# A MoBA attention and MoE MLP kernel: the written-out order of its operations, its buffer picks and its engine choices replaced

## The chip, the cores and the metric

The kernel runs on one core of one Trainium2 chip. The metric is the device time of one execution in microseconds (us). The kernel before was run three times: 254.47, 254.54 and 254.04 us, median 254.47. Its engines are TensorE (PE; its weight loads are listed apart as PEld), VectorE (DVE), ScalarE (ACT), GpSimd (POOL) and SyncE (SP), which here only issues DMAs. Each engine works through its own instruction queue in order; an instruction that waits holds up everything behind it on that engine.

## The reference

The inputs are q, k and v of shape 4 x 8 x 768 x 64 (batch, head, position, width) and the weights w_in (512 x 2048) and w_out (2048 x 512). Per batch and head there is an attention in which each position sees its own block of 64 keys and the blocks among its three best, by the product of its query with the mean of a block's keys:

```
k_rep = k.reshape(B, H, 12, 64, D).mean(axis=3)
gate  = where(causal by block, q . k_rep, -1e9)
mask  = (block in the best 3 of gate, or own block) and key <= query
attn  = softmax(where(mask, q . k / 8, -1e9))
x     = (attn @ v), heads side by side: 3072 x 512
h     = x @ w_in
g     = 0.5 h (1 + tanh(c (h + 0.044715 h^3)))
out   = g @ w_out
```

## The kernel before

The 32 heads are worked on as 16 pairs, p = 0 to 15; pair p belongs to batch b = p // 4. The kernel first describes its whole work as operations, each of which issues one or a few instructions on one engine, with the operations it depends on and the buffers it takes. They get numbers in the order in which they are described. Three written-out tables then say what becomes of them: ORDER is the sequence of the numbers in which the operations are issued, which is thus each engine's sequence too; BUFFER picks, for each buffer taken, one of the copies of its kind; ENGINE lists the operations that run on another engine than the first that they name. This is done at L215 to L225:

```python
engine = {n: e for e, ops in ENGINE.items() for n in ops}
picks = iter(BUFFER)
for n in ORDER:
    op = self.ops[n]
    for kind, key in op.takes:
        if key not in self.buf:
            self.buf[key] = self.kinds[kind][0][next(picks)]
    op.emit(engine.get(n, next(iter(op.engines))))
```

No planner runs when the kernel is built: the three tables are the schedule.

The work of a pair runs as follows.

- **Loads.** load (L371 to L398) brings keys, queries and values by SP, in two transfers for batch 0 and for all values (L387), in four of 32 columns each for the keys and queries of batches 1 to 3 (L393). Pair 0 has its own form, load_0 (L414 to L421): keys on SP's queue, queries on ScalarE's, each in two halves. The values are cast to 16 bit by GpSimd (cast_v, L358).
- **Weights.** load_w (L445 to L453) brings w_in and w_out in two halves each, issued by GpSimd. The first of these issues stands behind a small copy (L451) that needs pair 3's values to have landed. A small transfer on SP (hold, L1560) keeps the loads of batch 1 behind the landing of w_in.
- **Turning.** In batch 0, TensorE transposes keys (L538) and queries (L541) through PSUM, and copies and casts bring them back. In the other batches VectorE transposes 32 x 32 blocks (tr, L557) and a cast (q16 and kc, L356 on ScalarE, L360 on VectorE, L358 on GpSimd) makes them 16 bit.
- **Gate.** VectorE sums the keys of each block (ks, L614; the product ksb, L588 or L631, places them for two heads), TensorE multiplies them with the queries (gate, L680), and VectorE picks the best three (L696 to L717). The result is turned by TensorE or by a DMA (L749, L756) and copied (mc) into twelve extra rows below the queries (76 rows in all), with marker rows below the keys (fill, L513).
- **Scores.** TensorE makes the scores (L856 in batch 0, L1039 else), ScalarE their exponentials (L875, L1052), GpSimd clears what is not causal (L901, L1066), TensorE multiplies with the values and a column of ones (L924, L1078), VectorE divides (L942 and L943, L961 and L962). TensorE turns the result (ot, L981; a DMA at L986 for some) and a copy, otc, puts it into xT.

The work of a batch after its attention is the first product s1 with w_in (L1115, two matmuls to an operation), the gelu on ScalarE (L1127) and the second product with w_out. In batch 0 the second product is plain (s2_plain, L1315; stored at L1340). In batches 1 to 3 it has the form of Strassen with seven products of halves (L1365), whose sums VectorE makes (L1284 for the weights, L1302) and joins (L1414; stored at L1449 and L1458). Batch 3's first product also has this form for three of its column groups (prod, L1204): a product lies in a wide buffer of PSUM, of which there are two; keep (L356, L360) copies one half out of it, and plus (L1163) adds the other.

Around these, ORDER weaves one batch's products into the next batch's attention. Matmuls of zeros (warm, L1517) stand in front of the first work and at chosen places further on. ScalarE changes its table between exponential and gelu (L822).

Of the kernel before, what the change touches and what calls it, by code (L numbers as in the profile page):

```python
# [182 lines left out]
    "POOL": [  # L183
        337, 586, 587, 646, 647, 707, 708, 972, 973, 1035, 1036, 1097, 1159,
        1160, 1425, 1426, 1488, 1489, 1551, 1613]}


class Op:
# [1431 lines left out]
```

## Time and profile before

| | |
|---|---|
| runs | 254.47, 254.54, 254.04 us; median 254.47 |
| profiled execution | 253.93 us, of which span (first to last instruction) 252.2 us |
| granted TensorE clock | 1.000 |
| TensorE | 244.2 us, 97% of the span, 2484 instructions |
| VectorE | 188.8 us, 75%, 535 |
| ScalarE | 177.5 us, 70%, 226 |
| GpSimd | 84.0 us, 33%, 166 |
| DMA | 32.62 MB, 129 GB/s on average |

The profile is of one execution. A timeline row gives the start in us from the start of the span, the duration, engine, line, operation, what it writes and reads, the tile shape of a matmul, sizes and how many instructions the row groups; in brackets stands the idle time of the engine before it and what ended it. Rows of TensorE overlap, since its matmuls are pipelined: what one costs is read from the start of one to the start of the next. A row of the groups by line gives the busy time and the mean of one in ns, then the idle time before them and what ended it. A row of the windows gives the busy time in one stretch, engine by engine, with the instructions in brackets.

### The profile page before, as it was taken

What the parts mean: (1) busy time and instruction counts of PE and PEld (TensorE: products, weight loads), DVE (VectorE), ACT (ScalarE), POOL (GpSimd) and SP (SyncE); (2) the same over time, 40 slices, a digit from 0 to 9 for tenths busy, and PEclk for the clock granted to TensorE, in tenths of its full rate; (3) what the DMA queues carried; (4) which work ended last, traced back from release to release, by engine and by line L of the source; (5) the groups of instructions that cost most, each with busy time, mean ns of one, the idle gap of its engine ahead of it and who ended that gap; (6) DMA issues with size and microseconds to landing.
All of it is one profiled execution on the core that took longest, in us unless ns stands there. A gap on an engine that the chain in (4) does not pass through costs nothing.

```text
span 252.2 us, 6437 instructions
## 1 busy us (share of the span) xinstructions
PE 244.2 (97%) x2484; PEld 170.2 (67%) x2484; DVE 188.8 (75%) x535; ACT 177.5 (70%) x226; POOL 84.0 (33%) x166
## 2 busy tenths in 40 slices
PE   6899999999999999999999999999999999999993
PEld 4677776555555565565778887656777887666883
DVE  2679851034789999999997998999876585688954
ACT  2498978545899899867899795576999936656200
POOL 8657860011237657112147561210147500000000
PEclk9999999999999999999999999999999999999999
DMA  7998699999989987999899667184121330100023
GB/s 159 218 200 184 97 213 198 205 156 151 153 140 164 155 170 127 146 138 261 151 182 162 137 109 140 27 214 99 26 86 28 90 120 30 65 22 0 4 106 144
DMA packets 130927, 32.62 MB, mean 129 GB/s; under 512 B 124528, under 2 KB 126928, under 8 KB 130896
## 3 DMA queue, kind: packets, MB, share of 16 engines
q1 hardware_dynamic: 126160, 27.62, 62.8%
q0 software_dynamic: 3136, 4.19, 9.8%
q10 hardware_dynamic: 1600, 0.39, 0.8%
q8 instruction: 19, 0.31, 0.5%
q14 instruction: 12, 0.10, 0.1%
HBM read 27.26 MB, written 6.29 MB: 133 GB/s over the span
## 4 chain that ended last, share of the span: by engine, by line
PE 80%; SPq 8%; DMA 4%; DVE 3%; POOL 2%; issue 1%; DVEq 0%; POOLq 0%
PE wide L1115 27%; PE bank L1365 22%; PE wide L1039 9%; SPq L387 7%; PE bank L1315 6%; PE wide L1204 6%; PE bank L1078 5%; DMA vsd<-in_v_dram 2%; PE bank L680 2%; SPq L393 2%; DMA sd<-in_k_dram 1%; DMA G<-in_q_dram 1%; PE bank L924 1%; PE wide L856 1%; PE bank L981 1%
## 5 line engine op out<-in xcount | busy, mean ns | idle before, releaser
L1115 PE MATMUL wide<-xT,w_in 128*128 128x384 f16 x416 | 74.8, 326 | 0.0
L1052 ACT ACTIVATE ats<-wide 128x896 f16<-128x896 f32 x72 | 63.1, 915 | 5.8 <-PE wide L1039 3.8
L1127 ACT ACTIVATE G<-wide 128x768 f16<-128x768 f32 x52 | 42.0, 810 | 27.4 <-PE wide L1115 23.1
L1115 PEld LDWEIGHTS <-w_in 128*128 128x128 f16 x416 | 39.9, 98 | 26.9 <-issue 1.0
L1066 POOL TENSOR_SCALAR_AFFINE_SELECT ats<-ats 128x256 f16<-128x256 f16 x72 | 31.0, 443 | 51.1 <-ACT ats L1052 37.5
L1039 PE MATMUL wide<-qT,kT 76*128 76x512 f16 (+3 forms) x192 | 38.8, 305 | 0.0
L557 DVE STREAM_TRANSPOSE s<-sd 128x768 f32<-128x768 f32 x24 | 23.2, 971 | 14.2 <-DMA sd<-in_k_dram 12.9
L1365 PE MATMUL bank<-w_out,G 128*128 128x256 f16 x216 | 32.6, 272 | 0.0
L1365 PEld LDWEIGHTS <-G 128*128 128x128 f16 x288 | 26.9, 98 | 5.5
L1315 PE MATMUL bank<-w_out,G 128*128 128x512 f16 x96 | 28.8, 379 | 0.0
L358 POOL CAST kT<-s 64x768 f16<-64x768 f32 x20 | 16.9, 855 | 33.0 <-DVE s L557 32.4
L1414 DVE TENSOR_TENSOR osb<-bank,osb 128x512 f32<-128x512 f32 (+1 forms) x38 | 22.2, 592 | 4.7 <-PE bank L1365 4.1
L1078 PEld LDWEIGHTS <-ats 128*128 128x128 f16 x504 | 22.8, 98 | 4.2
L1078 PE MATMUL bank<-v,ats 128*128 128x65 f16 x504 | 24.9, 194 | 0.0
L1039 PEld LDWEIGHTS <-kT 76*128 76x128 f16 x192 | 17.2, 98 | 9.8 <-issue 0.3
L875 ACT ACTIVATE ats<-wide 128x1024 f16<-128x1024 f32 (+3 forms) x24 | 20.8, 916 | 3.2 <-PE wide L856 3.0
L1365 PEld LDWEIGHTS <-XS 128*128 128x128 f16 x216 | 20.1, 97 | 4.3
L1365 PE MATMUL bank<-TS,XS 128*128 128x256 f16 x144 | 22.6, 272 | 0.0
L358 POOL CAST v<-vsd 128x768 f16<-128x768 f32 x13 | 11.1, 858 | 22.9 <-DMA vsd<-in_v_dram 15.7
L962 DVE TENSOR_TENSOR xn<-bank,zr 128x384 f16<-128x384 f32 x24 | 13.4, 557 | 0.8
L712 DVE MAX8 sel<-sel 128x8 f32<-128x12 f32 x160 | 13.3, 157 | 0.6
L356 ACT CAST qT<-s 64x768 f16<-64x768 f32 x15 | 12.4, 830 | 0.3
(118 smaller groups left out, 352.8 us busy)
## 6 DMA issues: line engine op xcount, KB each, us to landing
out_dram<-osb SPq DMA_DIRECT2D x23, 256.0 KB
vsd<-in_v_dram SPq DMA_DIRECT2D x26, 192.0 KB
sd<-in_k_dram SPq DMA_DIRECT2D x48, 96.0 KB
sd<-in_q_dram SPq DMA_DIRECT2D x48, 96.0 KB
w_in<-in_moe_w_in_dram POOLq DMA_DIRECT2D x2, 1024.0 KB, 11.6
w_out<-in_moe_w_out_dram POOLq DMA_DIRECT2D x2, 1024.0 KB, 20.6
G<-in_k_dram SPq DMA_DIRECT2D x6, 192.0 KB
TS<-in_v_dram SPq DMA_DIRECT2D x6, 192.0 KB
```

Source lines behind the costliest of these rows:

```text
L358: nc.gpsimd.tensor_copy(out=out, in_=in_)
L557: nc.vector.transpose(out=T[key + "T32", p], in_=T[key, p].rearrange("p t j -> p (t j)"))
L875: nc.scalar.activation(out=T["at", u][:, :, 0:n], in_=plan.buf[("st",) + u].rearrange("p (h w) -> p h w", h=2)[:, :, 0:n], func=AF.Exp, bi ...
L1039: nc.tensor.matmul(st[:, x:e], kT16[i][h][0:76, s0:s0 + 128], qT16[i][h][0:76, s0 + (x - cb):s0 + (e - cb)], start=True, stop=True)
L1052: nc.scalar.activation(out=T["at", u][:, 0:n], in_=plan.buf[("st",) + u][:, 0:n], func=AF.Exp, bias=0.0, scale=SCALE)
L1066: nc.gpsimd.affine_select(out=dg, in_=dg, compare_op=ALU.is_ge, fill=0.0, base=0, pattern=[[0, 2], [1, 128]], channel_multiplier=-1)
L1078: nc.tensor.matmul(pvv[:, qc, 0:65], at[:, cb + (qc - jc) * 128: cb + (qc - jc + 1) * 128], v16[i][:, jc, h, :], start=(gi == 0 and jc == ...
L1115: nc.tensor.matmul(hps[:, 512 * e:512 * e + HALF], w_in16[:, ci, (2 * j + e) * 128: (2 * j + e + 1) * 128], T["xT", b][:, ci, HALF * h:HAL ...
L1127: nc.scalar.activation(out=G[:, :, h, j, :], in_=plan.buf["hps", b, j, h].rearrange("p (e w) -> p e w", e=2)[:, :, 0:HALF], func=AF.Gelu_a ...
L1315: nc.tensor.matmul(plan.buf["ops", b, ti], G[:, f % 2, 2 * ti // NC, f // 2, ti % (NC // 2) * 128:ti % (NC // 2) * 128 + 128], w_out16[:, ...
L1365: nc.tensor.matmul(dst[:, HD * h:HD * h + HD], FACT[m][0][:, j, t * 128:(t + 1) * 128], FACT[m][1][:, j, :], start=(clear and j == 0), sto ...
L1414: nc.vector.tensor_tensor(out=dst(), in0=src(), in1=other(), op=ALU.add)
```

## The change

The change replaces ORDER, BUFFER and ENGINE. Every function of the kernel stays as it is, and so does the set of operations, but for one matmul of zeros (1927), which is no longer issued: ORDER has 1666 entries after 1667. BUFFER has new picks for the new sequence.

The diff of ENGINE, whole:

```diff
     "ACT": [
-        67, 72, 74, 90, 99, 101, 110, 114, 119, 121, 139, 331, 345, 346,
-        348, 449, 467, 486, 504, 523, 541, 580, 598, 628, 654, 657, 716,
-        749, 857, 893, 929, 980, 981, 1043, 1044, 1105, 1106, 1167, 1168,
-        1202, 1346, 1497, 1558, 1620, 1668, 1674, 1677, 1698, 1707, 1727,
+        63, 67, 74, 99, 101, 114, 119, 121, 345, 346, 349, 449, 467, 486,
+        504, 523, 541, 594, 595, 628, 654, 657, 715, 716, 719, 749, 893,
+        980, 981, 1043, 1044, 1105, 1106, 1167, 1168, 1202, 1433, 1434,
+        1496, 1497, 1558, 1559, 1668, 1674, 1677, 1704, 1707, 1727, 1733,
         1736, 1786, 1822],
     "POOL": [
-        337, 586, 587, 646, 647, 707, 708, 972, 973, 1035, 1036, 1097, 1159,
-        1160, 1425, 1426, 1488, 1489, 1551, 1613]}
+        338, 586, 587, 646, 647, 707, 708, 972, 973, 1035, 1036, 1097, 1098,
+        1159, 1160, 1425, 1426, 1488, 1489, 1550, 1551, 1612, 1613]}
```

In words: casts of queries of pairs 5, 7, 12, 13 and 14 (594, 595, 715, 1433, 1434, 1496, 1559) go from VectorE to ScalarE, that of pair 15 (1620) the other way; casts of keys of pairs 10, 14 and 15 (1098, 1550, 1612) go from VectorE to GpSimd, and of pair 4 one goes each way (337, 338). Of the copies, 63, 349, 719, 1704 and 1733 go to ScalarE, and 72, 90, 110, 139, 331, 348, 580, 598, 857, 929, 1346 and 1698 to VectorE.

The first lines of ORDER (the rest is renewed in the same way):

```diff
-    4, 2, 0, 1890, 1891, 1892, 1893, 1894, 1895, 1896, 6, 1897, 15, 1898, 9,
-    1899, 1900, 1901, 12, 1, 1902, 62, 18, 71, 64, 195, 1903, 73, 72, 63,
-    75, 82, 1904, 22, 1905, 1906, 23, 76, 66, 1907, 31, 19, 74, 35, 77, 36,
+    5, 2, 1890, 6, 1891, 1892, 1893, 9, 15, 0, 1894, 1895, 1896, 1897, 12,
+    1898, 1899, 1900, 22, 1901, 1902, 1903, 23, 1904, 1905, 1906, 71, 72,
+    62, 73, 195, 64, 63, 82, 75, 76, 66, 1907, 3, 77, 1908, 74, 1, 18, 1909,
...
```

The moves that matter to a reader of the prediction:

- Pair 0's queries: 9 is the first half, 15 the second, both on ScalarE's queue. Before, 15 is issued ahead of 9; after, 9 ahead of 15.
- Numbers from 1890 on are the matmuls of zeros. Ahead of the first real matmul stand 13 of them before and 17 after; four fewer stand between the first score matmuls (194) and the first product.
- SP's loads: before, keys ahead of queries for pairs 1 and 2, and values of pair 2 ahead of those of pair 1; after, queries ahead of keys, and values of pair 1 ahead of those of pair 2. Pair 3's values come at the same place in both, behind the same loads. In batch 1's stage the loads of pairs 6 and 7 and of pairs 8 to 10 change places among each other; pair 7's keys and queries are issued ahead of more of the others, pair 6's values (639, 640) behind more of them.
- Of the first product, 393 and 406 stand ahead of 433, the first operation of the second product, before and behind it after.
- Nine operations of batch 0's second product move from ahead of batch 1's first scores to behind them.
- The gates of pairs 8 and 9 stand apart before and next to each other after. Gates of pairs 10 and 11 are together in both. Before, those of pairs 13, 14 and 12 form one group and pair 15's stands alone; after, 13 and 12 form one and 15 and 14 another.
- Around pair 7's gate, on VectorE: before, the normalisation 565 (pair 4) stands ahead of the transpose of pair 7's queries, and behind that transpose the cast 715 and then ksb; after, 715 is on ScalarE's queue, ksb stands ahead of the transpose, 565 behind it, and another normalisation of pair 4 (578) ahead of both.

296 rows, old and new, of tables (BUFFER, ORDER) are left out of this document.

## The prediction

> **What bounds the kernel now.** I read the busy shares and slices of the page, then its chain of waits, then the windows by stage, and last the timelines of the places where TensorE stands still.
>
> ```profile
> PE 244.2 (97%) x2484; PEld 170.2 (67%) x2484; DVE 188.8 (75%) x535; ACT 177.5 (70%) x226; POOL 84.0 (33%) x166
> ...
> PE   6899999999999999999999999999999999999993
> ...
> PE 80%; SPq 8%; DMA 4%; DVE 3%; POOL 2%; issue 1%; DVEq 0%; POOLq 0%
> ```
>
> TensorE is busy 97% of the span, is full from the third slice to the last but one, and holds 80% of the chain. The change keeps every operation but one warm-up matmul, so TensorE's work stays. A reordering can win only where TensorE waits, switches its tile shape or runs a filler. It can lose where an operand comes later than TensorE gets to it. The other engines decide that, and two stages are tight (columns: start:end, length, then busy time of each engine with its count).
>
> ```profile
> core 0: us, PE busy (x) PEld busy (x) DVE busy (x) ACT busy (x) POOL busy (x), PEclk, DMA share, GB/s
> 69.10:97.10 28.00, 27.52 (x314) 16.45 (x314) 26.22 (x78) 26.28 (x34) 15.32 (x30) 1.00 0.89 150
> 123.90:151.90 28.00, 28.00 (x348) 22.94 (x346) 25.83 (x50) 25.07 (x34) 15.54 (x30) 1.00 0.89 140
> ```
>
> These are the attention heads of batches 1 and 2. ScalarE is busy 26.28 and 25.07 of 28.00 us, VectorE 26.22 and 25.83. Yet TensorE lost .48 us in the one and nothing in the other.
>
> **The head.** The changed order issues the first half of pair 0's queries ahead of the second and puts four warm-up matmuls more in front of the first real one. It lets SP bring the queries of pairs 1 and 2 ahead of their keys.
>
> ```profile
> 6.77 0.52 PE L541 MATMUL bank<-identk,G 128*128 128x128 f32 x3 [1.47 <-DMA G<-in_q_dram]
> ...
> 10.71 0.28 PE L856 MATMUL wide<-XS,XS 64*128 64x256 f16 x2
> ```
>
> TensorE waited 1.47 us for a half of pair 0's queries. With the halves swapped, that half comes first, and I estimate the first scores (10.71) at about .7 us earlier: half of that wait, since the other half still lands last. Little of it can last, for the weights come by their own clock.
>
> ```profile
> 25.83 0.20 POOL L451 COPY after_in<-vsd 1x16 f32<-1x16 f32 x1 [0.79 <-DMA vsd<-in_v_dram]
> 26.36 1.66 POOL L453 DMA_DIRECT2D w_in<-in_moe_w_in_dram  x2 [0.34 <-issue]
> ...
> 28.66 1.78 POOL L453 DMA_DIRECT2D w_out<-in_moe_w_out_dram  x2
> ```
>
> ```profile
> DMA to landing us min/median/max: 18.2/20.6/23.0
> ```
>
> ```profile
> 39.93 0.27 PE L1517 MATMUL bank<-XS 128*128 128x256 f16 x1
> 40.04 2.76 PE L1115 MATMUL wide<-xT,w_in 128*128 128x384 f16 x16
> ...
> 47.68 0.38 PE L1315 MATMUL bank<-w_out,G 128*128 128x512 f16 x1
> 47.90 1.79 PE L1115 MATMUL wide<-xT,w_in 128*128 128x384 f16 x10
> ```
>
> The weights' issues wait for the values of pair 3 to land (25.83), which have the same bytes ahead of them on SP in both orders. The first half of w_out was issued at 28.66 and, by the view of that tile, landed 18.2 us later, at 46.86. Its first user (number 433) ran at 47.68, so .82 us was to spare. The change puts 433 ahead of 393 and 406, two operations of two first-product matmuls each: 16 matmuls take 2.76 us, so about .165 each and .65 for the four. That leaves .82 − .65 = .17. However fast the head becomes, only 0 to .17 us passes this point: I take −.10, the middle. Where the head becomes no faster the term is nothing. SP's other loads are reordered within the same stages with the same bytes: nothing by itself, hidden by the time for which a landed tile stands before its first cast; without that cover it would be a wait like the one at pair 7's gate below.
>
> **Gates merged.** Each group of gate matmuls (L680) uses a tile of another shape (128*32 beside 128*128). Before, pairs 8 and 9 were gated apart; now they stand together, as pairs 10 and 11 do in both.
>
> ```profile
> 94.39 0.38 PE L1315 MATMUL bank<-w_out,G 128*128 128x512 f16 x1
> 94.70 0.48 PE L680 MATMUL bank<-s,ksb 128*32 128x160 f32 x8
> 95.12 0.61 PE L1315 MATMUL bank<-w_out,G 128*128 128x512 f16 x2
> ```
>
> ```profile
> 115.06 0.75 PE L680 MATMUL bank<-s,ksb 128*32 128x160 f32 x16
> 115.75 1.47 PE L1115 MATMUL wide<-xT,w_in 128*128 128x384 f16 x8
> ```
>
> Start to start a lone gate takes 95.12 − 94.70 = .42, and the matmul ahead of it 94.70 − 94.39 = .31, against .22 where such a matmul is followed by its like (47.68 to 47.90): .51 for one, 1.02 for two. Merged, 115.75 − 115.06 = .69, with .09 ahead: .78. The saving is .24; I take −.22, bounds −.15 (without the switch) and −.24. Pair 9's keys must be there sooner for it, which the change allows by loading them earlier.
>
> **One filler fewer.** It stood between batch 1's heads; by the starts 39.93 and 40.04 a filler takes .11 us. −.11, or nothing where it filled a wait.
>
> **Pair 7's gate.** This is the .48 us that batch 1's stage lost.
>
> ```profile
> 84.27 0.50 PE L981 MATMUL bank<-ident,xn 128*128 128x128 f16 x6
> 85.25 0.48 PE L680 MATMUL bank<-s,ksb 128*32 128x160 f32 x8 [0.47 <-DVE ksb L631]
> ```
>
> ```profile
> 83.24 0.97 DVE L557 STREAM_TRANSPOSE s<-sd 128x768 f32<-128x768 f32 x1
> 84.24 0.65 DVE L360 CAST qT<-s 64x768 f16<-64x768 f32 x1
> 84.81 0.38 DVE L631 TENSOR_TENSOR ksb<-bmask,ks 128x32 f32<-128x32 f32 x1
> ...
> 85.45 0.56 DVE L962 TENSOR_TENSOR xn<-bank,zr 128x384 f16<-128x384 f32 x1
> ```
>
> On VectorE's in-order queue a cast of queries (.65) stood between the transpose (.97) and the small product ksb (.38) that the gate needs. The change gives that cast (715) to ScalarE, puts ksb ahead of the transpose, and has one normalisation of pair 4 (578) there in place of the other (565, .56 as in the last row), which goes behind it. The transpose is then the last of the chain and can end near 84.24 + .38 = 84.6, and TensorE is free for the gate at 85.25 − .47 = 84.8. So the wait goes: −.45, bounds 0 (the other normalisation stands on top of what was there, .56) and −.48. Late next is 565 itself, whose consumer is a transpose behind other matmuls.
>
> **The dual section.** In batch 3's first product by sums, a copy out of PSUM (1733) goes from VectorE to ScalarE.
>
> ```profile
> 227.02 0.38 PE L1365 MATMUL bank<-w_out,G 128*128 128x256 f16 x2
> 227.25 0.81 PE L1204 MATMUL wide<-xT,w_in 128*128 128x384 f16 x4
> 227.90 0.38 PE L1365 MATMUL bank<-w_out,G 128*128 128x256 f16 x2
> 228.30 0.81 PE L1204 MATMUL wide<-sd 128*128 128x384 f16 x4
> ```
>
> ```profile
> 227.29 0.96 DVE L360 COPY ats<-wide 128x768 f32<-128x768 f32 x1
> ```
>
> ```profile
> L356 ACT COPY ats<-wide 128x768 f32<-128x768 f32 x5 | 4.0, 799 | 2.4 <-PE wide L1204 2.4
> ```
>
> Two such matmuls take .23 from 227.02 to 227.25, but .40 from 227.90 to 228.30: TensorE waits about .17 for the wide buffer that the copy frees at 228.25. ScalarE makes the same copy in .80, .16 shorter, and VectorE comes to its next sum earlier. −.17, bounds 0 and −.19. Other copies and casts that change engines here (1704 to ScalarE, 1698 back) cancel.
>
> **Casts to other engines.** Batch 1's heads give ScalarE three casts of queries more (594, 595, 715) and one copy more (349), and take two away (348, 580); batch 2's give it three (1433, 1434, 1496) and take two small copies (857, 929).
>
> ```profile
> L1052 ACT ACTIVATE ats<-wide 128x896 f16<-128x896 f32 x72 | 63.1, 915 | 5.8 <-PE wide L1039 3.8 <-PE bank L1078 0.3 <-issue 0.2
> ...
> L356 ACT CAST qT<-s 64x768 f16<-64x768 f32 x15 | 12.4, 830 | 0.3
> ...
> L356 ACT COPY osb<-bank 128x512 f32<-128x512 f32 x6 | 3.5, 580 | 0.0
> ...
> L356 ACT COPY xT<-bank 128x768 f16<-128x768 f16 x4 | 3.2, 799 | 2.1 <-PE bank L981 2.1
> ...
> L356 ACT COPY osb<-bank 128x256 f32<-128x256 f32 x6 | 2.2, 368 | 1.7 <-PE bank L1365 1.7
> ```
>
> Batch 1: 3 × .83 + .58 − 2 × .80 = +1.47 against 28.00 − 26.28 = 1.72 us of idle time, and nine second-product matmuls (9 × .22 = 2.0 us) move from ahead of batch 1's first scores to behind them, which starts the exponentials some .8 us earlier, an estimate. Batch 2: 2.49 − .74 = +1.75 against 2.93. Behind each cast wait the exponentials, and behind those the causal selects on GpSimd and the products with the values. Before its exponentials ScalarE waited mostly for score matmuls (3.8 of 5.8 us), so the idle time follows TensorE's pace and can be used: nothing in the sum for it. GpSimd gets three casts of keys (busy 15.54 of 28.00 us): nothing, hidden by its idle half; without that, the selects queued behind each would be late.
>
> **New waits.** Every operand now meets TensorE at another time. No row tells which will be late. From below, batch 2's stage lost 0 us; from above, two waits like pair 7's, about 1.0. I take +.4, a little less than one such wait, because the old order had one in the two stages together.
>
> **Sum.** −.10 − .22 − .11 − .45 − .17 + .40 = −.65 on the profiled 253.93 (span 252.2 and 1.7 around it): 253.28. The median of the runs, 254.47, is .54 above the profiled one, so I say 253.8.
>
> **Rivals.** *A, ScalarE becomes the bound* (the side of a slower kernel): exponentials queued behind the added casts come late, score matmuls wait for wide buffers. It decides once less than .67 us of the idle time in batch 1 (1.47 − .8) or 1.75 us in batch 2 can be used. With a quarter usable (.43 and .73) it costs .24 + 1.02 = 1.26: 255.1. With none, 2.42: 256.2. For it speak 94% and 90% busy; against it, that waits for TensorE end most of the idle time.
>
> *B, w_out lands late.* Its margin in the new order is .17 us. The other half of w_out took 23.0 us against 18.2; if the first half is later by half of that spread, 2.4 − .17 = 2.2 us of waiting follow, less the −.10: 256.1. From a delay of about 1.3 us on it makes the kernel slower. GpSimd issues these transfers (28.66), and VectorE's products do stretch near GpSimd's work:
>
> ```profile
> 77.84 0.93 DVE L703 TENSOR_TENSOR sel<-sel,cgate 128x120 f32<-128x120 f32 x1
> ...
> 86.30 0.28 DVE L703 TENSOR_TENSOR sel<-sel,cgate 128x120 f32<-128x120 f32 x1
> ```
>
> The same product took .93 us once and .28 another time. Against B: both weights' issues are unmoved, and the bytes ahead of them are the same. The Trainium skill, "SBUF — State Buffer", in "SBUF: two separate sides", says that descriptors of a transfer issued from GpSimd are written by it, and that VectorE holding the port pair which the two share starves them. By that rule VectorE's reordered work around 28 us could delay the landing, and the time would be B's. By the rows of the issues, which took 1.66 and 1.78 us one behind the other with no gap but .34, this trace doesn't show it.
>
> *C, gains and new waits cancel*: pair 7's wait moves to another operand (+.45 on the forecast): 254.3.
>
> *D, no new wait at all*: .4 off the forecast, 253.4; with every other term at its best bound (−.07, −.02, −.03, −.02) 253.26.
>
> **How the numbers follow.** A measurement of this kernel tells about 0.2%, .5 us, from no change: faster is below 253.96, slower above 254.98. The forecast has .42 (its own range 253.4 to 254.3, three quarters of it below the bound: .33 faster, .09 same), D .11 (faster), C .18 (same), A .18 and B .11 (slower but for .01 of their mild ends). That gives faster .44, same .28, slower .28. The range 253.0 to 255.4 holds D with the runs' own spread (half of 254.04 to 254.54) below it, the forecast, C and the mild half of A; left out are A's upper half and B, .20 together.
>
> **What would show it.** Right: the first scores near 10.0 and 433 at 46.9 to 47.6; one gate group of 16 for pairs 8 and 9; no wait ahead of pair 7's gate; TensorE's start-to-start of .23 at the copy of the dual section; ScalarE's windows fuller by 1.5 to 1.8 with TensorE's at 28.0. Wrong: score matmuls waiting for exponentials, a wait for w_out before 433, or several waits for casts, ksb or normalisations in batches 1 to 3.

## The result, and the profile after

| | before | after |
|---|---|---|
| median of 22 runs each | 254.09 us | 253.62 us |
| lowest and highest | 253.58, 256.06 | 252.46, 254.11 |
| ratio of after to before | | .9967, 95% interval .9953 to .9982 |
| profiled execution, span | 253.93 us, 252.2 us | 254.11 us, 252.4 us |

The new order is faster by .33% (.18 to .47%). The means are .83 us apart (254.35 and 253.52), the medians .47: three executions of before at 255.57 to 256.06 and six of after below 253.3 pull the means apart. Its profiled execution is the slowest of its 22, so the two spans don't show the gain; where it lies is read from single places, and from further profiles below. Two executions of the experiments took far longer, 1416.64 us in head_only (its profiled one) and 317.12 us in rest_only; they are left out, and no trace of head_only is read. The page of the changed kernel first: the busy times, TensorE's slices, the chain.

```profile
PE 244.2 (97%) x2483; PEld 170.4 (68%) x2483; DVE 188.6 (75%) x533; ACT 178.5 (71%) x225; POOL 86.8 (34%) x169
...
PE   7898999999999999999999999999999999999993
...
PE 91%; DVE 4%; DMA 2%; issue 1%; ACTq 1%; ACT 0%; DVEq 0%
```

TensorE's work is what it was. Its waits, in the view that lists what it waited for (total us, times, longest), have moved to the head: the .5 us at pair 7's ksb (L631) is gone. Mask transposes (L749) and a ksb of batch 0 (L582) have 2.3 us, where before listed .3; the waits for pair 0's keys and queries fell from 1.9 to .8 us.

```profile
PE bank L749 <- DVE madd L717: 1.8, 3, 0.8
PE bank L1517 <- DVE bmask L285: 1.1, 1, 1.1
PE bank L541 <- DMA G<-in_q_dram: 0.8, 1, 0.8
PE bank L680 <- DVE ksb L582: 0.5, 1, 0.5
```

The windows of the two tight stages, same columns as before:

```profile
69.10:97.10 28.00, 27.96 (x307) 16.72 (x306) 24.41 (x76) 27.28 (x36) 16.29 (x32) 1.00 0.92 145
123.90:151.90 28.00, 28.00 (x355) 22.91 (x353) 25.19 (x48) 26.45 (x34) 15.61 (x29) 1.00 1.05 177
```

ScalarE went from 26.28 to 27.28 us of batch 1's 28 and TensorE still from 27.52 to 27.96: a ScalarE that is 97% busy did not become the bound. Its windows are fuller by 1.00 and 1.38 us, where the prediction had 1.5 to 1.8. VectorE fell from 26.22 to 24.41 us.

Pair 7's gate, in TensorE's and VectorE's timelines of the changed kernel:

```profile
85.14 0.38 PE L1078 MATMUL bank<-v,ats 128*128 128x65 f16 x7
85.45 0.48 PE L680 MATMUL bank<-s,ksb 128*32 128x160 f32 x8
```

```profile
83.34 0.36 DVE L631 TENSOR_TENSOR ksb<-bmask,ks 128x32 f32<-128x32 f32 x1
83.73 0.49 DVE L360 COPY qT<-bank 12x640 f16<-12x640 f16 x1
84.25 0.98 DVE L557 STREAM_TRANSPOSE s<-sd 128x768 f32<-128x768 f32 x1
85.26 0.20 DVE L961 RECIPROCAL zr<-bank 128x6 f32<-128x6 f32 x1
```

The transpose ends at 85.23, the gate starts at 85.45, with no idle time noted: the wait of .47 is gone. The merged gates and the dual section:

```profile
100.21 0.84 PE L680 MATMUL bank<-s,ksb 128*32 128x160 f32 x16
100.98 0.82 PE L1115 MATMUL wide<-xT,w_in 128*128 128x384 f16 x4
...
226.29 0.38 PE L1365 MATMUL bank<-w_out,G 128*128 128x256 f16 x2
226.73 0.81 PE L1204 MATMUL wide<-sd 128*128 128x384 f16 x4
...
228.25 0.38 PE L1365 MATMUL bank<-w_out,G 128*128 128x256 f16 x2
228.49 0.81 PE L1204 MATMUL wide<-sd 128*128 128x384 f16 x4
```

The two gates take .77 and not the .69 of pairs 10 and 11. At the copy 1733 TensorE now goes on after .24 us, .40 before; but one product earlier, where before had .33 (226.04 to 226.37), it is .44.

### The profile page after: what moved, and what is told of

It is laid out like the page before. It is cut to its first block, busy times and chain, and to the rows that moved or that the text cites. A ratio compares the mean times of both kernels' runs of the same rounds, so it can differ in the third digit from the quotient of the medians.

```text
span 252.4 us, 6423 instructions
## 1 busy us (share of the span) xinstructions
PE 244.2 (97%) x2483; PEld 170.4 (68%) x2483; DVE 188.6 (75%) x533; ACT 178.5 (71%) x225; POOL 86.8 (34%) x169
## 4 chain that ended last, share of the span: by engine, by line
PE 91%; DVE 4%; DMA 2%; issue 1%; ACTq 1%; ACT 0%; DVEq 0%
PE wide L1115 27%; PE bank L1365 22%; PE wide L1039 11%; PE bank L1315 8%; PE bank L1078 6%; PE wide L1204 5%; PE wide L856 3%; PE bank L680 2%; PE bank L924 2%; DMA G<-in_q_dram 2%; PE bank L541 1%; PE bank L749 1%; PE bank L981 1%; DVE sel L712 1%; DVE sel L713 1%
## 5 line engine op out<-in xcount | busy, mean ns | idle before, releaser
L1052 ACT ACTIVATE ats<-wide 128x896 f16<-128x896 f32 x72 | 62.0, 913 | 3.6 <-PE wide L1039 1.3
L1365 PE MATMUL bank<-w_out,G 128*128 128x256 f16 x216 | 31.9, 272 | 0.0
L1315 PE MATMUL bank<-w_out,G 128*128 128x512 f16 x96 | 28.1, 379 | 0.0
L1039 PEld LDWEIGHTS <-kT 76*128 76x128 f16 x192 | 17.3, 97 | 10.6 <-issue 0.5
L1078 PEld LDWEIGHTS <-ats 128*128 128x128 f16 x504 | 21.8, 97 | 3.6 <-POOL ats L1066 0.2
L358 POOL CAST kT<-s 64x768 f16<-64x768 f32 x23 | 19.5, 846 | 14.0 <-DVE s L557 13.2
L1078 PE MATMUL bank<-v,ats 128*128 128x65 f16 x504 | 24.1, 194 | 0.0
L356 ACT CAST qT<-s 64x768 f16<-64x768 f32 x21 | 17.4, 827 | 0.3
```

What stands on the lines that cost most here:

```text
L358: nc.gpsimd.tensor_copy(out=out, in_=in_)
L1039: nc.tensor.matmul(st[:, x:e], kT16[i][h][0:76, s0:s0 + 128], qT16[i][h][0:76, s0 + (x - cb):s0 + (e - cb)], start=True, stop=True)
L1052: nc.scalar.activation(out=T["at", u][:, 0:n], in_=plan.buf[("st",) + u][:, 0:n], func=AF.Exp, bias=0.0, scale=SCALE)
L1078: nc.tensor.matmul(pvv[:, qc, 0:65], at[:, cb + (qc - jc) * 128: cb + (qc - jc + 1) * 128], v16[i][:, jc, h, :], start=(gi == 0 and jc == ...
L1315: nc.tensor.matmul(plan.buf["ops", b, ti], G[:, f % 2, 2 * ti // NC, f // 2, ti % (NC // 2) * 128:ti % (NC // 2) * 128 + 128], w_out16[:, ...
L1365: nc.tensor.matmul(dst[:, HD * h:HD * h + HD], FACT[m][0][:, j, t * 128:(t + 1) * 128], FACT[m][1][:, j, :], start=(clear and j == 0), sto ...
```

## The experiments

Each kernel is the old or the new one with an edit to ORDER and ENGINE (and BUFFER's picks where two orders are spliced). The tables of the experiments are six lines shorter, so L625 there is L631 here, and so on. All ratios are against the kernel before, run beside them. BUFFER's picks were not tried by themselves.

**Where the gain lies: the head or the rest.** Up to 433, the first operation of the second product, old and new order hold the same operations but seven, so that either part can be put in front of the other.

```diff
 after_again:  the changed kernel
 head_only:    new order of what stands ahead of 433, then the old order
 rest_only:    old order of the same, then the new order
```

> The changed kernel once more, for a second profile. Theory (the gain lies behind the head: pair 7's gate .45, gates of pairs 8 and 9 merged .22, a filler .11, the dual section a little, about .8 us in all, and the head gives or takes up to .9 us from one execution to the next): about .997 of before, no wait ahead of pair 7's gate, and number 433 anywhere from 46.9 to 47.8. Rival (the gain is the head's, the rest is nothing): .997 too, but only in executions in which 433 comes earlier than before's 47.68.

> The new order, picks and engines for what stands ahead of 433, the old ones from there on (393 and 406 ahead of 433, as before). Theory: no gain, .999 to 1.003 of before, pair 7's wait of .47 back at its place. Rival: the gain is all here, .997.

> The old head, the new order, picks and engines from 433 on. Theory: about .997 (-.8 us), or more than the changed kernel if its head costs. Rival: 1.000.

Measured: after_again .9968 (.9947 to .9989), head_only .9998 (.9975 to 1.0021), rest_only .9972 (.9953 to .9992). The gain is behind 433; the new head gives nothing on average, to the .2% that these runs tell. From the start of 433 to the last matmul the traces have 200.44 us before, with .65 us of first product (393 and 406) already done that the new order still has to do: 201.09 on equal work. After has 200.59, after_again 200.59, rest_only 200.53: .50 to .56 us less, nearly the same in each execution. Of the terms of this gain only pair 7's gate is tried by itself below; the others are read from the traces.

**Pair 7's gate undone.**

```diff
 order on VectorE (after):  ... 709 658 711 565 ...   715 on ScalarE
-709 658 711 565
+658 711 715 709 565
 ENGINE["ACT"]
-715,
```

> The changed kernel with the cast 715 back on VectorE, behind the transpose of pair 7's queries, and ksb behind that cast. Theory: the gate of pair 7 waits again, .4 to .5 us, and all of it passes to the end: the changed kernel's time + .45, .9985 of before. Rival (another operand would have been late anyway, or later slack takes it up): the changed kernel's time, .997.

Measured 1.0058 (1.0036 to 1.0080), +2.1 us on the changed kernel and not +.45. Two places of VectorE's timeline in this kernel, what GpSimd did beside them, and TensorE behind them:

```profile
84.63 1.15 DVE L354 CAST qT<-s 64x768 f16<-64x768 f32 x1
...
93.69 1.94 DVE L625 TENSOR_TENSOR ksb<-bmask,ks 128x32 f32<-128x32 f32 x1
```

```profile
84.55 0.82 POOL L352 CAST kT<-s 64x768 f16<-64x768 f32 x1
...
92.90 0.82 POOL L352 CAST kT<-s 64x768 f16<-64x768 f32 x1
93.67 0.77 POOL L1060 TENSOR_SCALAR_AFFINE_SELECT ats<-ats 128x256 f16<-128x256 f16 x2
94.40 0.82 POOL L352 CAST v<-vsd 128x768 f16<-128x768 f32 x1
95.18 0.40 POOL L1060 TENSOR_SCALAR_AFFINE_SELECT ats<-ats 128x256 f16<-128x256 f16 x1
95.78 0.78 POOL L1060 TENSOR_SCALAR_AFFINE_SELECT ats<-ats 128x256 f16<-128x256 f16 x2 [0.20 <-ACT ats L1046]
```

```profile
85.94 0.48 PE L674 MATMUL bank<-s,ksb 128*32 128x160 f32 x8 [0.69 <-DVE ksb L625]
...
98.10 0.37 PE L1072 MATMUL bank<-v,ats 128*128 128x65 f16 x7 [1.00 <-DVE xn L956]
```

The cast took 1.15 us beside a cast on GpSimd (.65 in the old kernel, where a select ran there), so the gate waited .69. Then VectorE came .7 us later to pair 8's ksb, which in the changed kernel takes .32, and here 1.94: from 93.69 to 95.63, as long as GpSimd worked without a gap (to 95.58). What was queued behind it on VectorE, a normalisation among it, came late, and TensorE waited 1.00 us more. These two waits are 1.69 of the 1.93 us by which 433 to the last matmul grew (200.59 to 202.52). One cast of .65 us, with ksb behind it, moved the end by 2.1.

**Is it GpSimd's run?** The same kernel, with one of GpSimd's casts moved out of that run into an idle stretch ahead of it.

```diff
 order (p7_undone), GpSimd's part
-676 972 684 728 704 732
+704 676 972 684 728 732
```

> The run before with 715 back on VectorE (1.0058 of before), and GpSimd's cast of pair 7's values (704) moved ahead of the select 676, out of its unbroken run of five operations from 93.68 to 95.58 us. Theory: VectorE's ksb of pair 8 took 1.94 us because it stood behind that run, and the 1.0 us for which TensorE waited at 98.1 came from it; with a gap at 94.4 ksb takes .8 or less, the wait is gone, and the time falls by about 1.0, to 1.002. Rival (ksb was late for its operands or VectorE was simply behind by its extra cast): ksb as long as before, 1.006.

Measured 1.0007 (.9992 to 1.0022), 1.3 us less than p7_undone. In its VectorE timeline:

```profile
92.55 0.44 DVE L625 TENSOR_TENSOR ksb<-bmask,ks 128x32 f32<-128x32 f32 x1
```

ksb takes .44, TensorE's wait of 1.00 is gone, and 433 to the last matmul takes 201.35 us after p7_undone's 202.52: 1.17 less. So the place of GpSimd's cast made the product late, as the theory says. But it did not wait for a gap here: it ended at 92.99, and GpSimd's selects ran on from 92.54 to 93.30, the second starting at 92.90. It got in where one operation of GpSimd followed another directly, and so it did in the next run; in p7_undone it didn't at three such places. What lets a waiting product in is open.

**Pair 7's cast and ksb alone, in the old kernel.**

```diff
 order on VectorE (before)
-711 715 709
+709 711            715 on ScalarE, behind 580
```

> The old kernel with two things changed: the cast 715 on ScalarE, behind 580, and ksb 709 ahead of the transpose 711 on VectorE. Theory (the wait at pair 7's gate is lost time by itself): no wait there and -.45 us, .998 of before. Rival (ScalarE has no room at that place: its next exponentials start .4 to .6 us later and score matmuls wait for them): the gate's wait gone, and the same time or more, 1.000 to 1.001.

Measured .9994 (.9976 to 1.0012). The gate's wait fell from .47 to .33 only, and what ended it was now the transpose:

```profile
85.09 0.48 PE L674 MATMUL bank<-s,ksb 128*32 128x160 f32 x8 [0.33 <-DVE s L551]
```

```profile
83.28 0.82 POOL L352 CAST v<-vsd 128x768 f16<-128x768 f32 x1
```

```profile
83.35 0.80 DVE L625 TENSOR_TENSOR ksb<-bmask,ks 128x32 f32<-128x32 f32 x1
84.07 0.97 DVE L551 STREAM_TRANSPOSE s<-sd 128x768 f32<-128x768 f32 x1
```

ksb, put ahead of the transpose, took .80 and not .38: a cast of GpSimd ran from 83.28 to 84.10, and ksb ended .05 us behind it. Neither theory: the wait is .14 us shorter, 433 to the last matmul .18 (200.26 after 200.44), and no new wait for ScalarE shows. The ratio can't tell so little. That the changed kernel loses the whole wait needs the rest of its order. In rest_only, which has the old head too, VectorE's rows at this place are:

```profile
82.49 0.37 DVE L625 TENSOR_TENSOR ksb<-bmask,ks 128x32 f32<-128x32 f32 x1
...
83.41 0.98 DVE L551 STREAM_TRANSPOSE s<-sd 128x768 f32<-128x768 f32 x1
```

The transpose ends at 84.39 and not at 85.04, and .43 of these .65 us are ksb's shorter time; TensorE is free for the gate at 84.60 and doesn't wait.

**How near ScalarE is to being the bound.** Three kernels change the changed kernel's ENGINE alone.

```diff
 act_stress: ENGINE["ACT"] + 597, 598, 655
 act_plus:   ENGINE["ACT"] + 658
 act_minus:  ENGINE["ACT"] - 594, 595     (back on VectorE)
```

> The changed kernel with one cast and two copies of batch 1's heads more on ScalarE (655, 597, 598; .83 + 2 x .68 = 2.2 us; the changed kernel left ScalarE .72 us idle in the 28 us of that stage). Rival A of the prediction says that ScalarE decides once its idle time is used up: 2.2 - .7 = 1.5 us more at least, 1.003 of before or over. Against it: VectorE, relieved of 1.5 us, pays for it, and the time stays at .997 to .999.

> The changed kernel with one copy more on ScalarE (658, .68 us, pair 6's mask rows at about 84 us, where ScalarE's exponentials follow each other with gaps of under .1 us). Rival A of the prediction in its small form: the exponentials behind it are .6 us later and TensorE waits .4 to .7 us for a wide buffer; .999 to 1.000 of before. Against it: VectorE, relieved of .49 us, reaches the transpose for pair 7's gate sooner and nothing is lost; .997.

> The changed kernel with the casts of pair 5's queries (594, 595) back on VectorE. Theory (ScalarE is nearly full, but VectorE is the scarcer one: each VectorE product that comes late can fall behind a run of GpSimd): TensorE's two small waits for exponentials at 74.7 and 91.6 us (.13 and .2 in the changed kernel) shrink, and waits for VectorE of .5 us or more come in their place; .999 to 1.002. Rival (ScalarE is the tighter one there): .996.

Measured: act_stress 1.0110 (1.0079 to 1.0140), act_plus .9979 (.9959 to .9999), act_minus .9989 (.9971 to 1.0008). From 433 to the last matmul: act_plus 200.96 and act_minus 201.11, against 200.59. For the small ones the traces tell more than the intervals, which overlap with the changed kernel's and with each other. act_plus has new waits of .10 and .29 us at score matmuls that start at 86.43 and 87.95. The changed kernel has two small ones of .13 and .20 us (at 74.7 and 91.6 in after_again; in the first profile the score matmuls behind them start at 75.06 and 92.03, each .05 us behind the end of an exponential). The second:

```profile
91.06 0.92 ACT L1052 ACTIVATE ats<-wide 128x896 f16<-128x896 f32 x1
```

```profile
92.03 0.54 PE L1039 MATMUL wide<-qT,kT 76*128 76x512 f16 x3
```

act_minus loses the first and keeps the second, and has a wait for VectorE's cast:

```profile
77.38 0.54 PE L1033 MATMUL wide<-qT,kT 76*128 76x512 f16 x3 [0.39 <-DVE qT L354]
```

Both directions cost, by these traces. In act_stress it isn't the sum of ScalarE's work that decides: it is busy 26.41 us of the same 28, the changed kernel's 27.28, though the fixed window holds less of the delayed stage. ScalarE's rows and TensorE's:

```profile
74.01 0.68 ACT L350 COPY qT<-bank 12x640 f16<-12x640 f16 x1 [0.93 <-PE bank L743]
74.70 0.83 ACT L350 CAST qT<-s 64x768 f16<-64x768 f32 x1
75.56 1.73 ACT L1046 ACTIVATE ats<-wide 128x896 f16<-128x896 f32 x2
```

```profile
76.53 0.54 PE L1033 MATMUL wide<-qT,kT 76*128 76x512 f16 x3 [1.69 <-ACT ats L1046]
```

The added copy (598) waits .93 us for a transpose of TensorE, a cast and two exponentials wait behind it in ScalarE's queue, and TensorE waits 1.69 us for them. In all the kernel is 3.1 us longer than the changed one from 433 on (203.72 and 200.59), 3.6 by the ratios, where the expectation had at least 1.5.

**The head: one race with two outcomes.** The changed kernel's times fall in two groups: 6 of 22 from 252.46 to 253.22, the others from 253.56 on (of after_again's 12, two lie at 252.7, one at 253.37, the others from 253.62 on). In the changed kernel's three profiles the time is 206.4 us more than the start of 433 (253.63 and 47.28, 253.89 and 47.49, 254.11 and 47.75), so that the spread lies ahead of 433. One profile with the new head had 433 at 46.35, the seven others at 47.3 to 47.8. The early one (undone_cast_moved), VectorE and GpSimd:

```profile
16.22 0.55 DVE L570 TENSOR_REDUCE ks<-bank 128x6 f32<-128x384 f32 x1
16.80 0.17 DVE L576 TENSOR_TENSOR ksb<-bmask,ks 128x12 f32<-128x12 f32 x1
...
17.91 0.17 DVE L576 TENSOR_TENSOR ksb<-bmask,ks 128x12 f32<-128x12 f32 x1
```

```profile
16.81 0.86 POOL L352 CAST v<-G 128x768 f16<-128x768 f32 x1 [2.21 <-DMA G<-in_v_dram]
```

and a late one, the changed kernel's first profile:

```profile
17.04 0.65 DVE L582 TENSOR_TENSOR ksb<-bmask,ks 128x12 f32<-128x12 f32 x1
...
18.58 0.60 DVE L582 TENSOR_TENSOR ksb<-bmask,ks 128x12 f32<-128x12 f32 x1
```

```profile
16.83 0.83 POOL L358 CAST v<-G 128x768 f16<-128x768 f32 x1 [2.00 <-DMA G<-in_v_dram]
17.61 0.77 POOL L901 TENSOR_SCALAR_AFFINE_SELECT ats<-ats 128x256 f16<-128x256 f16 x2
18.33 0.82 POOL L358 CAST XS<-s 128x768 f16<-128x768 f32 x1
```

GpSimd's cast starts when pair 0's values land. If ksb 115 starts ahead of it, by .01 us in the early profile, it takes .17 us; if behind, .65, and later products then meet GpSimd's next operations (ksb 111 .60, the selection 124 2.75 and not 1.87 us). The head is 1.1 us later. In all eight late profiles (the eighth is head_fix, below) ksb starts .03 to .41 us behind the cast's start and ends within .04 us of the cast's end, so the sooner it comes behind the start, the longer it takes (.83 to .43 us). In the old head the two ksb of this place start at 17.3 to 18.2 and take .20 to .23 us in all four profiles that have it.

```diff
 head_fix: order (after), ENGINE
-120 95 87 94 196 201 121 32 102
+95 102 120 87 196 201 94 121 32        94 on ScalarE
```

> The changed kernel with pair 1's gate (102, and its ksb 95) ahead of a transposition of pair 2's queries (120), and the copy 94 on ScalarE, so that VectorE comes to ksb 115 some .1 us earlier. Theory: in the head this product races GpSimd's cast of pair 0's values (30), which starts when they land; where it comes behind the cast's start it takes 1.2 instead of .76 us, two more products get behind GpSimd's selects, and the head is 1.1 us later (433 at 47.5 and not at 46.4; 6 of the changed kernel's 22 executions lie below 253.3 us, the others above 253.5). With the .1 us more executions win the race: median 252.7 to 253.3, .995 of before, or, if .1 us is too little, 253.6 with more executions below 253.3. Rival (the two groups of times come from the landings of the weights): no change, 253.6, .997, a quarter of the executions below 253.3.

> One more look at the changed kernel's head. Theory of the race: either VectorE's ksb 115 takes about .76 us and 433 starts by 46.5, or it takes 1.2 and more and 433 starts at 47.4 to 47.8. A ksb of .76 with 433 after 47.3, or the other way round, speaks against it.

Measured: head_fix .9994 (.9976 to 1.0012), median 254.07, 2 of 12 executions under 253.3. Its edit did not do what it was for: the gate then waited for its own operands, VectorE came to the sum ahead of ksb 115 at 16.43 (16.21 to 16.45 without the edit), and lost the race again (cast at 16.99, product 1.41 us with its sum, 433 at 47.74). So it says nothing on what winning is worth. after_look: 433 at 47.28, ksb 115 with its sum 1.20 us, which agrees with the race, but that 433 was expected at 47.4 or later. The rival, the weights' landing, doesn't fit: the lead is there at the first transpose of results (L981 at 28.41 in the early profile, 29.48 to 29.95 in the late ones), 8 us ahead of the first product with weights. That the race makes the 1.1 us rests on one early profile against eight late ones; no run forced a win.

**A version that fills the small waits.**

```diff
 best_try: order (rest_only)
+528 ahead of 735, 494 ahead of 557, 1789 behind 1827, 1792 behind 1779
```

> The old head with the new rest, and four matmul operations moved into waits of .1 to .2 us that its trace shows (528 ahead of 735, 494 ahead of 557, 1789 behind 1827, 1792 behind 1779). Theory: each filled wait is time won, .5 to .7 us together beyond .9972, so .995. Rival: the waits are the pace of ScalarE and VectorE and come back at the next matmul that needs them, .997.

Measured .9969 (.9949 to .9990): rest_only's .9972. From 433 to the last matmul it takes 200.45 us against 200.53. Of rest_only's waits those that end at 74.2, 225.9 and 230.7 are gone, that at 91.2 now stands behind 528 (.20 again), and two of .18 and .15 have come, which end at 229.08 and 235.60: the rival's account. It is within the interval of the changed kernel; no run beat it clearly.

## Why the prediction was right

The forecast was 253.8 us, .65 less than before by its own sum; measured were 253.62, .47 less by the medians, and a ratio that stands for .84 less. The median that the sum started from, 254.47 of three runs, is .38 above that of the 22. Point by point:

- **TensorE bounds, only waits can be won.** Right: its busy time is 244.2 us in both.
- **Head, −.10.** The size agrees on average (head_only .9998, to .2%), but by luck, for the working was wrong. The first scores came at 10.85, not at 10.0: the queries did land earlier, but then TensorE waited .74 us for a mask of VectorE's (madd). And 433 was not held to 46.86. The prediction had the weights' issues unmoved, but w_out's first half was issued at 28.66 before and at 30.70 after, 2 us later, and landed at the same 46.8; in other executions it landed at 46.0, and in one of them 433 ran at 46.35. Mostly the head arrived later than that, at 47.3 to 47.8, most likely by the race.
- **Gates merged, −.22.** Right in kind, mis-sized: .41 + .09 twice before, .77 + .09 after, −.14. From the first gate's start to the second's it is .36 us, where pairs 10 and 11 have .30, and the second then takes .41 against .39. What held the second no row names.
- **Filler, −.11.** The fillers behind 433 take .61 us before and .49 after.
- **Pair 7's gate, −.45.** The wait is gone as forecast, and with it .53 us. The reason was incomplete: the cast and ksb by themselves gained .14 in the old order (p7_alone), because ksb, beside a cast of GpSimd, took .80. The durations that were added up (.65, .38) hold only for what GpSimd does at that moment.
- **Dual section, −.17.** The wait at the copy went (.40 to .24), but one of .11 came at the product before it: with the small rest of the section −.08 net. The bound 0 had been there for this.
- **Casts on ScalarE at nothing, new waits +.40.** The new waits are .13 at 74.7 and .20 at 91.6, .33 together, and both are score matmuls behind exponentials: the beginning of rival A. The first goes with pair 5's casts (act_minus), the second doesn't. The +.40 was taken from the old order's one wait and not worked out from the new order, so its size is partly luck. By the traces one copy more costs .37 (act_plus) and two casts fewer .52 (act_minus).

The measured terms behind 433 sum to −.14 − .12 − .53 − .08 + .33 = −.54, against −.50 to −.56 read from 433 to the end. Where TensorE can gain, and that pair 7's gate is the largest gain, was right; that the sum came within some .1 of this is helped by terms that were off by up to .10 to either side.

Rival A was real and near, but its condition was wrong: not idle time used up, since ScalarE went to 97% and only .33 us of waits came, but a long operation or a waiting copy ahead of an exponential that TensorE needs next. Rival B did not come: w_out landed no later. The Trainium skill's rule that it rested on ("SBUF — State Buffer", "SBUF: two separate sides": VectorE can keep GpSimd from writing descriptors) shows in no run here: w_out's two issues took .88 and .90 us in all 13 profiles read. Another rule of that page does show: its section "Who interferes with whom" says that a VectorE instruction with two SBUF inputs contends with a GpSimd instruction that reads SBUF, and ksb, with two such inputs, took 1.94 us and .44 us by GpSimd's order alone. Rival C (a wait moves to another operand) is what p7_alone showed for .33 of the .47 us, and best_try in its small waits; in the changed kernel it did not come.

## What to carry to other kernels

Where TensorE is full, a reordering is worth what its waits are worth, and single waits can be read and summed to a few tenths. But on VectorE and GpSimd a duration belongs to a moment: before a small product with two inputs in memory is moved, look at what GpSimd runs there, and how long it runs without a gap. An operation that waits in the queue of a nearly full engine can cost more than the operation itself (a copy of .68 us, and TensorE waited 1.69). Where run times fall in two groups, look for a place where two engines race within some tenths of a us: one profile shows only one outcome.

## What was not expected of the hardware

- A product of 128 x 32 elements on VectorE took 1.94 us beside 1.9 us of unbroken GpSimd work, .32 and .44 us where it got in behind the first operation, and .17 us beside an idle GpSimd (85.71 in p7_undone). The new order does not lessen this over the whole kernel, it moves it: the selection's product (L703) takes 298 ns on average after and 436 before, but ksb (L631) 301 after and 204 before. Before, then after:

```profile
L703 DVE TENSOR_TENSOR sel<-sel,cgate 128x120 f32<-128x120 f32 x15 | 6.5, 436 | 0.3
L631 DVE TENSOR_TENSOR ksb<-bmask,ks 128x32 f32<-128x32 f32 x12 | 2.4, 204 | 0.1
```

```profile
L703 DVE TENSOR_TENSOR sel<-sel,cgate 128x120 f32<-128x120 f32 x15 | 4.5, 298 | 0.3
L631 DVE TENSOR_TENSOR ksb<-bmask,ks 128x32 f32<-128x32 f32 x12 | 3.5, 301 | 0.1
```

- A cast from 32 to 16 bit of 64 x 768 on VectorE, one input only, took 1.15 us beside a cast on GpSimd and .55 us alone (.65 in the old order, beside a select). Both stretched ones end .41 us behind the end of the GpSimd operation that ran when they started (85.37 to 85.78, 84.48 to 84.89).
- A weight transfer issued 2 us later landed at the same time (28.66 + 18.2 and 30.70 + 16.1 us); in all 13 profiles read this half landed at 45.9 to 46.9, issued at 28.6 to 31.0.
